# A planned attention and feed-forward kernel: urgencies corrected by two tables, two buffers laid out by block, and a plan that knows PSUM turns and the port

## The chip, the cores and the metric

The kernel runs on one core of one Trainium2 chip. The metric is device time in microseconds of that core; a run is one execution of the whole program. Engines are named as in the profile: PE (TensorE, the matrix engine), DVE (VectorE), ACT (ScalarE), POOL (GpSimd) and SP, whose queue issues every DMA of this kernel.

## What is computed

Chunked attention, whose output is the input of a gated feed-forward layer. Shapes: 8 batches, 8 heads, 576 positions, head size 64, so 4608 rows of 512; chunks of 64 positions; the feed-forward layer is 1024 wide.

```python
scores = q_chunk @ k_chunk.T / 8              # 64x64 for each chunk and head
attn = exp(scores - max) ; attn /= sum + 1e-9
x = attn @ v_chunk                            # heads side by side: rows of 512
h = maximum(x @ w_in, 0)                      # 512 -> 1024
conv[s] = cw[0]*h[s-1] + cw[1]*h[s] + cw[2]*h[s+1]   # zero beyond a batch
out = (h * sigmoid(conv)) @ w_out             # 1024 -> 512
```

The weights w_in, conv_w and w_out come as 64-bit floats; q, k and v as 32-bit floats.

## The kernel before

**Split products.** Each large product is made of three matrix products of shortened 32-bit numbers: high by high, high by low, low by high. So w_in, w_out, x and the gated g each exist as a pair of tiles in SBUF (`wi_h`/`wi_l`, `wo_h`/`wo_l`, `x_h`/`x_l`, `g_h`/`g_l`).

**Weights.** A 64-bit weight arrives as two 32-bit words in one of six raw slots (named `qk` in the profile, since rows of q and k use the same slots). The chain `split` turns one 512 KB piece into its high and low part: on DVE `w_mask` (L334), `w_rest` (L343), `w_low` (L347), `w_sign` (L352) or `w_one` (L358), and `w_pow` (L369); on ACT `w_bias` (L339), and `w_hi` (L362) where POOL doesn't make the high part with `w_hi_one` (L365); then mostly `w_lo_big` on POOL (L377) and `w_lo_copy` on ACT (L380). There are 8 pieces of w_in, 8 of w_out and a small one for conv_w. Before the change a piece of w_in is all 512 rows by 128 columns.

**Attention.** 36 tiles of 128 rows (two chunks). For each: rows of q and k are turned (`t_pe` on PE, L143, and `t_copy` on ACT, L147, for the first 9 tiles; `t_dve` on DVE, L152, for the others); `scores` on PE (L162); `s_max` (L172) and `s_sub` (L176) on DVE; `s_exp` on ACT (L181); `s_sum`, `s_eps`, `s_rec` on DVE (L185, L188, L191); `s_norm` on POOL (L194); `p_pe` (L201) and `p_copy` (L206); `attn_v` on PE (L214); then `x_hi` on ACT (L238) and `x_lo` on DVE (L242) write x. Scores and attention output share one PSUM tile, `sx_ps`, of two banks: scores lie in the first half of each bank, the output in the second half. The tile framework lets PE write a bank and DVE or ACT read it only one after the other.

**Feed-forward.** 16 units of 288 rows (half a batch). For each unit and each of 8 blocks of 128 columns: `mm1` on PE (L252, 12 matmuls over 290 columns; three PSUM buffers `h_ps`), then `h_relu`, `c_mid`, `c_sig` and `g_hi` on ACT (L258, L263, L278, L290), `c_left`, `c_right`, `c_mul` on DVE (L267, L273, L281) and `g_lo` on POOL (L294). x is a ring of three units. `mm2` on PE (L305) adds, for each of 36 output tiles, 8 steps of 3 matmuls; `o_copy` (L310) and `o_store` follow. Exp and sigmoid need different tables in ACT, so the profile shows table loads at L181 and L278.

**The order.** Nothing runs in the order in which it is written. Every piece of work is a `step` with an engine, an estimated cost, a key (its urgency), the steps it comes after, and the buffers that it takes and frees. A planner in the kernel's own Python (L567 to L650) plays the steps out engine by engine: among the ready steps of an engine, those that could start within 0.15 us of the earliest are candidates, and the lowest key wins. The steps are then issued in the planned order, and a dependency from each instruction to the one before it on its engine fixes that order. On the chip every engine works through its own list in that order and waits at each step for what the step needs.

The planner's DVE and POOL steps marked `port` share a port: when the other engine holds it, the planner before lengthens the step's cost, after the step is picked. It doesn't know that scores and attention output take turns in the two banks of `sx_ps`.

Of the kernel before, what the change touches and what calls it, by code (L numbers as in the profile page):

```python
# [30 lines left out]
def attn_ffn(ctx: ExitStack, tc: tile.TileContext, q, k, v, w_in, conv_w, w_out, out):  # L31
# [48 lines left out]
    wi_h = const.tile([P, KT, DF], F32R, name="wi_h")  # L80
    wi_l = const.tile([P, KT, DF], F32R, name="wi_l")
# [139 lines left out]
    def x_views(st, t, x):  # L221

        xv = sx[:, :, G * C:2 * G * C].rearrange("p s (g i) -> p g s i", i=C)
        parts = []
        for s in range(2):
            b, t0 = chunk(2 * t + s)
            for half, lo, hi in ((0, 0, HS + 2), (1, HS - 2, S)):
                i, j = max(lo, t0), min(hi, t0 + C)
                if i < j:
                    parts.append((s, i - t0, j - i, XU * ((2 * b + half) % NX) + i - lo))  # L230
        if [p[1:3] for p in parts] == [(0, C)] * 2 and parts[1][3] == parts[0][3] + C:
            o = parts[0][3]
# [12 lines left out]
    def mm1(st, u, f):  # L245

        o = XU * (u % NX)
        st["h"] = h_ps = ps_h.tile([P, 512], F32, name="h_ps")
        n = 0
        for wt, xt in ((wi_h, x_h), (wi_h, x_l), (wi_l, x_h)):  # L250
            for kt in range(KT):
                nc.tensor.matmul(  # L252
                    h_ps[:, 0:XU], lhsT=wt[:, kt, P * f:P * f + P], rhs=xt[:, kt, o:o + XU],
                    start=n == 0, stop=n == 3 * KT - 1)
                n += 1
# [180 lines left out]
    def att(t, key, load_key, exps, writes):  # L436
# [150 lines left out]
    while any(ready.values()):  # L587
        best = None
        for e, cand in ready.items():
            picks = []  # L590
# [94 lines left out]
```

## Time and profile before

| | us |
|---|---|
| median of 3 runs | 554.38 |
| lowest, highest | 553.79, 557.0 |
| the profiled execution, device time | 554.14 |
| its span, first to last instruction | 552.4 |

A profile shows one execution. The span is shorter than the device time by what lies around it, 1.74 us. "Busy" is the share of time in which an engine had an instruction of the kind; PE's weight loads are kept apart as PEld. A group row gives a line, engine, operation, output and inputs, the count, the total and mean time, and the idle time of the engine just before the group with what ended it. PE's matmuls overlap, so the time that one costs is the distance between two starts, not its own length: the length holds the way through the array too.

Three stages can be told apart. In the first there is no `mm1`; in the second the weights are still being split; from about 109 us on all weights are ready, and PE alternates between `mm1`, `mm2` and short excursions to the attention of later tiles.

### The profile page before, as it was taken

How to read it: one execution, taken by the hardware profiler on the slowest of the kernel's cores; microseconds unless marked ns; L12 is line 12 of the kernel's file. 1: busy time of each engine (PE TensorE's matmuls, PEld its weight loads, DVE VectorE, ACT ScalarE, POOL GpSimd, SP SyncE). 2: the span in 40 equal slices, each digit the busy share in tenths (PEclk: the TensorE clock that was granted, in tenths of full speed). 3: DMA queues.
4: the chain of work that ended last, by engine and by line, in shares of the span. 5: the costliest groups of instructions: out<-in, count | busy, mean ns of one | idle time of the engine just before them, and what ended most of it. 6: DMA issues, size and time to landing. Idle time of an engine off the chain costs nothing.

```text
span 552.4 us, 12919 instructions
## 1 busy us (share of the span) xinstructions
PE 507.9 (92%) x4921; PEld 435.8 (79%) x4921; DVE 373.8 (68%) x760; ACT 365.6 (66%) x819; POOL 183.2 (33%) x250
## 2 busy tenths in 40 slices
PE   3567678899999999999999999999999999999997
PEld 2456567788888878887888889797888888788985
DVE  4898979866868477475777656675877656655530
ACT  3558977767794667757594845767685845768641
POOL 0454644632341323322341421232342422232420
PEclk9979979999999999999999999999999999999999
DMA  8997650145324555423355551333352101000001
GB/s 191 243 222 208 165 118 1 40 96 93 64 48 106 90 121 107 99 58 72 82 95 103 106 106 50 58 80 70 81 104 68 39 20 40 1 20 21 21 38 58
DMA packets 185314, 47.03 MB, mean 85 GB/s; under 512 B 175500, under 2 KB 179620, under 8 KB 185252
## 3 DMA queue, kind: packets, MB, share of 16 engines
q1 hardware_dynamic: 185252, 46.20, 37.9%
q8 instruction: 39, 0.64, 0.5%
q14 instruction: 23, 0.19, 0.1%
HBM read 36.72 MB, written 9.44 MB: 84 GB/s over the span
## 4 chain that ended last, share of the span: by engine, by line
PE 74%; DVE 10%; ACT 8%; issue 2%; POOL 2%; DMA 2%; SPq 2%; POOLq 0%; ACTq 0%; DVEq 0%
PE o_ps L305 32%; PE h_ps L252 29%; PE sx_ps L214 4%; PE sx_ps L162 4%; PE pt_ps L201 3%; ACT L181 3%; POOL e L194 2%; DMA qk<-in_k 2%; DVE z L185 2%; ACT e L181 1%; PE h_ps L143 1%; DVE wv L347 1%; ACT c L263 1%; ACT h_ps L258 1%; ACT x_h L238 1%
## 5 line engine op out<-in xcount | busy, mean ns | idle before, releaser
L294 POOL TENSOR_TENSOR g_l<-c,g_h 128x288 fp32r<-128x288 f32 (+8 forms) x184 | 113.4, 630 | 245.4 <-ACT g_h L290 231.1
L305 PE MATMUL o_ps<-wo_h,g_h 128*128 128x512 f32 x288 | 120.4, 418 | 0.0
L305 PE MATMUL o_ps<-wo_l,g_h 128*128 128x512 f32 x288 | 113.6, 394 | 4.2 <-ACT wo_l L380 4.2
L267 DVE SCALAR_TENSOR_TENSOR c<-h_ps,cw,c 128x288 f32<-128x288 f32 (+1 forms) x128 | 65.1, 509 | 72.2 <-ACT c L263 72.2
L305 PE MATMUL o_ps<-wo_h,g_l 128*128 128x512 f32 x288 | 113.8, 395 | 0.0
L252 PE MATMUL h_ps<-x_h,wi_h 128*128 128x290 f32 x512 | 91.5, 301 | 5.3 <-DVE c L281 5.3
L252 PEld LDWEIGHTS h_ps<-x_h,wi_h 128*128 128x128 f32 x512 | 81.7, 191 | 16.5 <-DVE c L281 4.0
L278 ACT ACTIVATE c<-c 128x288 f32<-128x288 f32 x128 | 55.7, 444 | 57.4 <-DVE c L273 56.1
L252 PE MATMUL h_ps<-x_l,wi_h 128*128 128x290 f32 x512 | 91.1, 301 | 0.0
L252 PE MATMUL h_ps<-x_h,wi_l 128*128 128x290 f32 x512 | 90.1, 298 | 0.0
L281 DVE TENSOR_TENSOR c<-h_ps,c 128x288 f32<-128x288 f32 x128 | 56.9, 452 | 34.6 <-ACT c L278 34.0
L252 PEld LDWEIGHTS h_ps<-x_l,wi_h 128*128 128x128 f32 x512 | 76.7, 191 | 0.4 <-DVE x_l L242 0.3
L252 PEld LDWEIGHTS h_ps<-x_h,wi_l 128*128 128x128 f32 x512 | 76.5, 191 | 0.0
L290 ACT CAST g_h<-c 128x288 fp32r<-128x288 f32 (+8 forms) x184 | 59.4, 358 | 24.5 <-DVE c L281 23.0
L263 ACT ACTIVATE c<-h_ps,cw 128x288 f32<-128x288 f32 x128 | 64.0, 500 | 9.3 <-POOL g_l L294 0.4
L258 ACT ACTIVATE h_ps<-h_ps 128x290 f32<-128x290 f32 x128 | 50.8, 397 | 29.1 <-PE h_ps L252 27.9
L273 DVE SCALAR_TENSOR_TENSOR c<-h_ps,cw,c 128x287 f32<-128x287 f32 (+1 forms) x128 | 66.1, 517 | 4.2
L305 PEld LDWEIGHTS o_ps<-wo_h,g_l 128*128 128x128 f32 x288 | 54.3, 188 | 12.4
L305 PEld LDWEIGHTS o_ps<-wo_l,g_h 128*128 128x128 f32 x288 | 54.4, 189 | 10.4 <-ACT wo_l L380 5.2
L305 PEld LDWEIGHTS o_ps<-wo_h,g_h 128*128 128x128 f32 x288 | 54.4, 189 | 7.5
L194 POOL TENSOR_TENSOR e<-e,z 128x512 f32<-128x512 f32 x36 | 37.9, 1052 | 57.3 <-DVE z L191 42.1
L214 PEld LDWEIGHTS sx_ps<-pT,v 64*64 64x64 f32 x1152 | 21.8, 143 | 20.6 <-issue 8.0
(53 smaller groups left out, 549.5 us busy)
## 6 DMA issues: line engine op xcount, KB each, us to landing
v<-in_v SPq DMA_DIRECT2D x144, 64.0 KB, 2.7
out<-o_sb SPq DMA_DIRECT2D x36, 256.0 KB, 2.2
qk<-in_q SPq DMA_DIRECT2D x96, 48.0 KB, 2.3
qk<-in_k SPq DMA_DIRECT2D x96, 48.0 KB, 2.3
qk<-in_moe_w_in SPq DMA_DIRECT2D x8, 512.0 KB, 5.2
qk<-in_moe_w_out SPq DMA_DIRECT2D x8, 512.0 KB, 5.3
qk<-in_q SPq DMA_DIRECT2D x96, 24.0 KB, 1.9
qk<-in_k SPq DMA_DIRECT2D x96, 24.0 KB, 1.9
```

Source lines behind the costliest of these rows:

```text
L194: nc.gpsimd.tensor_tensor(out=st["e"], in0=st["e"], in1=st["z"].rearrange("p (h o) -> p h o", o=1).broadcast_to([P, H, C]), op=ALU.mult)
L214: nc.tensor.matmul(x_ps[D * hp:D * hp + D, s, C * g:C * g + C], lhsT=st["v"][j0:j0 + C, g, s, :], rhs=st["pT"][j0:j0 + C, g, C * s:C * s + C],
L252: nc.tensor.matmul(h_ps[:, 0:XU], lhsT=wt[:, kt, P * f:P * f + P], rhs=xt[:, kt, o:o + XU], start=n == 0, stop=n == 3 * KT - 1)
L258: nc.scalar.activation(out=st["h"][:, 0:XU], in_=st["h"][:, 0:XU], func=AF.Relu)
L263: nc.scalar.mul(out=st["c"], in_=st["h"][:, i0:i0 + HS], mul=cw[:, FT + f:FT + f + 1])
L267: nc.vector.scalar_tensor_tensor(out=c[:, a:HS], in0=st["h"][:, i0 + a - 1:i0 + HS - 1], scalar=cw[:, f:f + 1], in1=c[:, a:HS], op0=ALU.mu ...
L273: nc.vector.scalar_tensor_tensor(out=c[:, 0:b], in0=st["h"][:, i0 + 1:i0 + 1 + b], scalar=cw[:, 2 * FT + f:2 * FT + f + 1], in1=c[:, 0:b], ...
L278: nc.scalar.activation(out=st["c"], in_=st["c"], func=AF.Sigmoid)
L281: nc.vector.tensor_tensor(out=st["c"], in0=st["h"][:, st["i0"]:st["i0"] + HS], in1=st["c"], op=ALU.mult)
L290: nc.scalar.copy(out=g_h[:, f, gs], in_=st["c"][:, cs])
L294: nc.gpsimd.tensor_tensor(out=g_l[:, f, gs], in0=st["c"][:, cs], in1=g_h[:, f, gs].bitcast(F32), op=ALU.subtract)
L305: nc.tensor.matmul(st["o"], lhsT=gt[:, f, o:o + P], rhs=wt[:, f, :], start=f == 0 and n == 0, stop=f == FT - 1 and n == 2)
```

## The change

The added and removed code works at five places.

1. *Urgencies.* After all steps are made, two tables are added to the keys: `by_step` by the function's name, and `by_chain` by the chain of steps that share a state (one tile, one block, one weight piece). A search over plans made the numbers; a row of such a table says nothing by itself.
2. *The planner's rules.* A step on the shared port now starts only when the other engine has let go of the port (it waits in the plan, and another step may be picked). A step in the bank pair "sx" waits until the other engines' steps in that pair have ended. The window of candidates is 0.6 us instead of 0.15, and starting late costs 32 key points for each us. The first ACT step pays for a table load, and only ACT steps change the loaded table. Some costs of loads are raised.
3. *x by units.* `x_h` and `x_l` go from (4 row groups, 3 units x 290) to (3 units, 4 row groups, 290), so that what belongs to a unit lies together. Two chunks are written by one instruction only where both lie in one unit.
4. *w_in by blocks.* `wi_h` and `wi_l` go from (4, 1024) to (4 block pairs, 4, 256). A piece of w_in is now half of the rows by 256 columns, so two pieces are needed before the two blocks of a pair can start.
5. Loads, results and arithmetic are otherwise the same.

The core of the diff:

```diff
-    x_h = const.tile([P, KT, NX * XU], F32R, name="x_h")
+    x_h = const.tile([P, NX, KT, XU], F32R, name="x_h")
-    wi_h = const.tile([P, KT, DF], F32R, name="wi_h")
+    wi_h = const.tile([P, FT // 2, KT, 2 * P], F32R, name="wi_h")
...
-    src_i = [w_in.rearrange("(k p) f -> p k f", p=P)[:, :, 2 * P * f:2 * P * f + 2 * P] for f in range(FT)]
+    src_i = [w_in.rearrange("(k p) f -> p k f", p=P)[:, 2 * (n % 2):2 * (n % 2) + 2, 4 * P * (n // 2):4 * P * (n // 2) + 4 * P] for n in range(FT)]
...
+        for f in (n - n % 2, n - n % 2 + 1):
+            wi_done[f] = wi_done.get(f, []) + list(ends)
...
+    by_step = {
+        "w_bias": 3, "w_rest": 1.5, "w_sign": 1, "w_pow": -1.5, "w_hi": 5, "w_lo": 2.5, "w_one": 0.5, "w_hi_one": 1,
...
+    by_chain = [
+        -27, -43, -2, -2, -3, 12, 14, 1, -9, -107, 2, 2, 7, 5, 1, 0, 1, 11, -3, -1, -1, -7, -4, 11, -10, -9, 3, 1, 4,
...
+        s["key"] += by_step.get(name, 0.0) + by_chain[chains.setdefault(a, len(chains))] / 2
...
+                    if s["port"]:
+                        t = max(t, port[other[e]] - share[e])
+                    for o, until_ in bank.get(s["bank"], {}).items():
+                        if o != e:
+                            t = max(t, until_ + late[e])
...
-                t, _, i = min((p for p in picks if p[0] <= t + 0.15), key=lambda p: p[1])
+                t, _, i = min((p for p in picks if p[0] <= t + 0.6), key=lambda p: p[1] + 32 * (p[0] - t))
...
-            cost += max(0.0, port[other] - t - (0.2 if e == "DVE" else 0.137))
```

How this moves instructions shows at three places. The rows are in the order of one engine's list. Line numbers between 76 and 242 of the kernel before are one higher after the change.

The first is PE's list after the fourth unit, around the attention of tiles 12 to 14: L201 is `p_pe`, L214 `attn_v`, L162 `scores`, L305 a third of an `mm2` step, L252 a third of an `mm1`. Before, from `p_pe` of tile 12 on:

```order
L201 MATMUL pt_ps<-ident,e 128x128 x4
L305 MATMUL o_ps<-wo_h,g_h 128x512
L305 MATMUL o_ps<-wo_l,g_h 128x512
L305 MATMUL o_ps<-wo_h,g_l 128x512
L214 MATMUL sx_ps<-pT,v 64x64 x16
L201 MATMUL pt_ps<-ident,e 128x128 x4
L162 MATMUL sx_ps<-kT,qT 64x64 x16
L305 MATMUL o_ps<-wo_h,g_h 128x512
L305 MATMUL o_ps<-wo_l,g_h 128x512
L305 MATMUL o_ps<-wo_h,g_l 128x512
L214 MATMUL sx_ps<-pT,v 64x64 x16
```

After, from `attn_v` of tile 12 on (`scores` of tile 14 and `p_pe` of tile 12 stand three `mm2` steps earlier):

```order
L215 MATMUL sx_ps<-pT,v 64x64 x16
L202 MATMUL pt_ps<-ident,e 128x128 x4
L252 MATMUL h_ps<-x_h,wi_h 128x290 x4
L252 MATMUL h_ps<-x_l,wi_h 128x290 x4
L252 MATMUL h_ps<-x_h,wi_l 128x290 x4
L163 MATMUL sx_ps<-kT,qT 64x64 x16
L215 MATMUL sx_ps<-pT,v 64x64 x16
L252 MATMUL h_ps<-x_h,wi_h 128x290 x4
L252 MATMUL h_ps<-x_l,wi_h 128x290 x4
L252 MATMUL h_ps<-x_h,wi_l 128x290 x4
```

Between `attn_v` of one tile and `scores` of another there was only a `p_pe`, and between those `scores` and the next `attn_v` one `mm2` step; now a whole `mm1` lies between the first two, and `scores` and `attn_v` stand back to back.

The second is DVE's list at the first `mm1` blocks, while weights are split: L334, L343, L347, L358 and L369 are the weight chain; L172 is `s_max`, L176 `s_sub`, L185 `s_sum`, L267 and L273 `c_left` and `c_right`. Before:

```order
L172 TENSOR_REDUCE m<-sx_ps 128x8
L176 TENSOR_TENSOR e<-sx_ps,m 128x2x4x64
L369 TENSOR_SCALAR we<-wi_h 128x512
L334 TENSOR_SCALAR o_sb<-qk 128x512
L343 TENSOR_SCALAR wv<-qk 128x512
L267 SCALAR_TENSOR_TENSOR c<-h_ps,cw,c 128x287
L273 SCALAR_TENSOR_TENSOR c<-h_ps,cw,c 128x288
```

And the same stretch after:

```order
L173 TENSOR_REDUCE m<-sx_ps 128x8
L334 TENSOR_SCALAR o_sb<-qk 128x512
L358 TENSOR_SCALAR ws<-qk 128x512
L369 TENSOR_SCALAR we<-wi_h 128x512
L177 TENSOR_TENSOR e<-sx_ps,m 128x2x4x64
L267 SCALAR_TENSOR_TENSOR c<-h_ps,cw,c 128x287
L273 SCALAR_TENSOR_TENSOR c<-h_ps,cw,c 128x288
L186 TENSOR_REDUCE z<-e 128x8
L343 TENSOR_SCALAR wv<-qk 128x512
L369 TENSOR_SCALAR we<-wi_h 128x512
```

`w_rest` (L343) stood right behind `w_mask` (L334) and `w_pow`; now `s_sub`, `c_left`, `c_right` and `s_sum`, none of them marked for the port, stand ahead of it.

The third is the head of SP's list, the first loads. Before:

```order
L322 DMA qk<-in_moe_w_in 128x4x256
L103 DMA qk<-in_q 128x8x64
L103 DMA qk<-in_k 128x8x64
L135 DMA v<-in_v 64x4x64 x4
L322 DMA qk<-in_moe_w_in 128x4x256
L103 DMA qk<-in_q 128x8x64
```

After:

```order
L322 DMA qk<-in_moe_w_in 128x2x512 x2
L322 DMA qk<-in_moe_conv_w 24x256
L104 DMA qk<-in_q 128x8x64
L104 DMA qk<-in_k 128x8x64
L136 DMA v<-in_v 64x4x64 x4
L104 DMA qk<-in_q 128x8x64
```

Two pieces of w_in and conv_w now go ahead of the first rows of q, where one piece of w_in went before.

More of the change, by code (lines that the diff above doesn't have):

```diff
@@ L64, in attn_ffn, with step @@
     steps = []
-    def step(eng, cost, key, fn, args=(), after=(), take=(), free=(), lag=0.0, table=None, port=False):
+    def step(eng, cost, key, fn, args=(), after=(), take=(), free=(), lag=0.0, table=None, port=False, bank=None):
         s = dict(eng=eng, cost=cost, key=key, fn=fn, args=args, after=[a for a in after if a], take=take, free=free,
-                 lag=lag, table=table, port=port)
+                 lag=lag, table=table, port=port, bank=bank)
         steps.append(s)
@@ L454, in att @@
         tt[0]["after"] += [before["T"]] if t else []
-        s = step("PE", 0.47, key, scores, (st,), tt + [before.get("s")], take=["s"], free=["qT", "kT"])
+        s = step("PE", 0.47, key, scores, (st,), tt + [before.get("s")], take=["s"], free=["qT", "kT"], bank="sx")
         before.update(v=ldv, T=tt[1], s=s)
-        s = step("DVE", 0.69, key, s_max, (st,), [s], take=["m"])
-        s = step("DVE", 0.68, key, s_sub, (st,), [s], take=["e"], free=["m", "s"])
+        s = step("DVE", 0.69, key, s_max, (st,), [s], take=["m"], bank="sx")
+        s = step("DVE", 0.68, key, s_sub, (st,), [s], take=["e"], free=["m", "s"], bank="sx")
         exps.append(s)
@@ L467, in att @@
         s = step("ACT", 0.59, key + 12, p_copy, (st,), [s], take=["pT"], free=["pt"])
-        s = step("PE", 0.47, key + 14, attn_v, (st,), [s, ldv], take=["x"], free=["pT", "v"])
+        s = step("PE", 0.47, key + 14, attn_v, (st,), [s, ldv], take=["x"], free=["pT", "v"], bank="sx")
         n = len(x_views(st, t, x_h)) - 1
-        s = step("ACT", 0.58 + 0.15 * n, key + 14, x_hi, (st, t), [s] + writes)
-        return step("DVE", 0.69 + 0.1 * n, key + 14, x_lo, (st, t), [s], free=["x"])
+        s = step("ACT", 0.58 + 0.15 * n, key + 14, x_hi, (st, t), [s] + writes, bank="sx")
+        return step("DVE", 0.69 + 0.1 * n, key + 14, x_lo, (st, t), [s], free=["x"], bank="sx")
     group_loads, before = {}, {}
@@ L560, in attn_ffn @@
             step("SP", 0.5, key + 2, o_store, (st, t), [s], free=["o_sb"], lag=0.8)
+    by_step = {
+        "w_bias": 3, "w_rest": 1.5, "w_sign": 1, "w_pow": -1.5, "w_hi": 5, "w_lo": 2.5, "w_one": 0.5, "w_hi_one": 1,
+        "w_lo_copy": -1, "c_sum": 11, "c_pe": -1, "c_copy": 8.5, "load_rows": -0.5, "t_pe": 3, "t_copy": -3, "scores":
+        -2.5, "s_sub": 5, "s_exp": 1, "s_sum": 1, "s_eps": -0.5, "s_rec": -1, "s_norm": 4.5, "p_pe": 2.5, "p_copy": 7.5,
+        "attn_v": 2.5, "x_lo": 4.5, "h_relu": 3.5, "c_left": 1.5, "c_right": 0.5, "c_sig": 0.5, "c_mul": 1.5, "g_hi":
+        4.5, "g_lo": 9, "o_copy": -6, "o_store": 4, "load_group": -2, "load_part": 5, "t_dve": 8
+    }
+    by_chain = [
[9 rows of a table added]
+    ]
+    chains = {}
+    for s in steps:
+        a, name = s["args"][0] if s["args"] else None, s["fn"].__name__
+        a = id(a) if isinstance(a, dict) else ("load" if name.startswith("load") else name, a)
+        s["key"] += by_step.get(name, 0.0) + by_chain[chains.setdefault(a, len(chains))] / 2
     early = {"DVE": 0.083, "ACT": 0.092, "PE": 0.0, "POOL": -0.075, "SP": -0.05}
@@ L577, in attn_ffn @@
     free_at["SP"] = 0.7
-    port = {"DVE": 0.0, "POOL": 0.0}
-    dma_free, table, pe_f32 = 0.0, "exp", False
+    port, other, share = {"DVE": 0.0, "POOL": 0.0}, {"DVE": "POOL", "POOL": "DVE"}, {"DVE": 0.2, "POOL": 0.137}
+    dma_free, table, pe_f32, bank = 0.0, None, False, {}
     left = [len(a) for a in befores]
@@ L617, in attn_ffn @@
         s, cost = steps[i], steps[i]["cost"]
-        table = s["table"] or table
+        if e == "ACT":
+            table = s["table"] or table or "exp"
         if e == "PE":
```

36 lines of the change are left out of this document (18 added, 18 removed), and 8 rows, old and new, of the table by_chain.

## The prediction

> **What bounds the kernel now.** I read the page's first part and then the busy time by stage. The stages end at the first `mm1` (39.4 us), at the last weight operation of DVE (108.8) and at the last `mm1` (529.5). The columns are the stretch, its length, and busy time with instruction count of PE, PEld, DVE, ACT and POOL, then granted clock, DMA share and GB/s.
>
> ```profile
> PE 507.9 (92%) x4921; PEld 435.8 (79%) x4921; DVE 373.8 (68%) x760; ACT 365.6 (66%) x819; POOL 183.2 (33%) x250
> ...
> 0.00:39.40 39.40, 20.52 (x277) 15.59 (x278) 29.07 (x60) 19.56 (x35) 13.30 (x17) 0.95 0.91 218
> 39.40:108.80 69.40, 54.56 (x542) 47.34 (x541) 61.93 (x119) 54.83 (x111) 38.52 (x34) 0.93 0.46 113
> 108.80:529.50 420.70, 413.54 (x4023) 357.36 (x4022) 280.81 (x579) 286.24 (x661) 129.22 (x196) 1.00 0.34 70
> ```
>
> In the second stage DVE is busy for 61.93 of 69.40 us while PE idles for 14.8: DVE's weight chains set the pace there. In the third PE is busy for 413.54 of 420.70 and bounds the time. So the change is worth something in two ways: less DVE time lost before 108.8, and less PE time lost after it. How much PE loses in the third stage the busy share hides, since pipelined matmuls overlap. I take the counts there, and the distance between starts.
>
> ```profile
> L305 PE MATMUL o_ps<-wo_h,g_h 128*128 128x512 f32 x247 | 103.6, 419 | 0.0
> ...
> L252 PE MATMUL h_ps<-x_l,wi_h 128*128 128x290 f32 x444 | 78.1, 298 | 0.0
> ...
> L214 PE MATMUL sx_ps<-pT,v 64*64 64x64 f32 x928 | 20.2, 224 | 3.8 <-issue 3.1 <-ACT pT L206 0.7
> L162 PE MATMUL sx_ps<-kT,qT 64*64 64x64 f32 x896 | 19.4, 224 | 0.6
> L201 PE MATMUL pt_ps<-ident,e 128*128 128x128 f32 x116 | 18.8, 285 | 0.9
> ```
>
> The chain that ended last gives one `mm2` step (3 matmuls) as 19.25/28 = 0.69 us and one `mm1` (12) as 3.23/2 = 1.61.
>
> ```profile
> 509.81 3.23 PE h_ps L252 x24
> ...
> 529.56 19.25 PE o_ps L305 x84
> ```
>
> PE's timeline around a lone `scores` shows what an excursion from the wide matmuls to attention costs.
>
> ```profile
> 210.05 0.40 PE L305 MATMUL o_ps<-wo_l,g_h 128*128 128x512 f32 x1
> 210.29 0.40 PE L305 MATMUL o_ps<-wo_h,g_l 128*128 128x512 f32 x1
> 210.62 0.69 PE L162 MATMUL sx_ps<-kT,qT 64*64 64x64 f32 x32
> 211.24 0.51 PE L305 MATMUL o_ps<-wo_h,g_h 128*128 128x512 f32 x1
> 211.58 0.40 PE L305 MATMUL o_ps<-wo_l,g_h 128*128 128x512 f32 x1
> ```
>
> One mm2 matmul takes 0.69/3 = 0.23, so `scores` starts 0.10 late (0.33 after the start before it); it takes 0.62, and the matmul behind it 0.34 instead of 0.23. An excursion costs 0.21 beyond its own work.
>
> The third stage then holds 444/12 = 37 times three kinds, that is 111 `mm1`, 247 `mm2` steps, 29 `attn_v` (928/32), 28 `scores` and 29 `p_pe`: 179 + 170 + 18 + 17 + 10 (a `p_pe` at 0.35, the distance of two starts below), and about 1 for one last transpose, makes 395. Of 420.7 us, about 25 are lost. PE's list has 66 excursions from the 17th `mm1` on: 66 x 0.21 = 13.9. The other 11 or so are stalls, and this timeline of all engines shows the commonest, a turn in the PSUM banks of `sx_ps`:
>
> ```profile
> 199.48 0.69 PE L214 MATMUL sx_ps<-pT,v 64*64 64x64 f32 x32
> 200.11 0.66 PE L201 MATMUL pt_ps<-ident,e 128*128 128x128 f32 x4
> 200.25 0.59 ACT L238 CAST x_h<-sx_ps 128x512 fp32r<-128x512 f32 x1 [0.41 <-PE sx_ps L214]
> 200.89 0.69 PE L162 MATMUL sx_ps<-kT,qT 64*64 64x64 f32 x32
> ...
> 202.09 0.39 PE L305 MATMUL o_ps<-wo_h,g_l 128*128 128x512 f32 x1
> 202.33 0.68 DVE L172 TENSOR_REDUCE m<-sx_ps 128x8 f32<-128x512 f32 x1
> ...
> 203.11 0.69 PE L214 MATMUL sx_ps<-pT,v 64*64 64x64 f32 x32 [0.63 <-issue]
> ```
>
> `scores` could have started at 200.11 + 0.35 + 0.10 = 200.56; it starts at 200.89, when `x_hi` has left the bank (200.84). The next `attn_v` could have started at 202.32; it starts at 203.11, behind `s_max` (203.01). One such knot costs 0.33 + 0.79 = 1.12 us.
>
> **The change part by part.** The sum is made against the profiled execution, 554.14 us; the median of the runs is 554.38, 0.24 more.
>
> *Bank turns known to the plan.* The list before has five knots of this kind (tiles 12, 16, 23, 25 and 32); the list after has one `attn_v` as close behind `scores` (one 0.69 step), worth 0.8 as above, and two at 1.39 us of work, just short of what `s_max` and its like take twice (0.68 each, and the starts between), worth 0.1 each. Gain 5 x 1.12 - 1.0 = 4.6. Now `scores` often stands right behind `attn_v`: `x_hi` waits 0.62 longer, queued behind it on ACT are `p_copy` and conv work, and the next unit's first `mm1` waits for x. That `mm1` now mostly stands 2.9 us of PE work behind the unit's last `attn_v`, against 2.1 before, so the longer wait is covered.
>
> *Fewer excursions.* 66 become 48: 18 x 0.21 = 3.8.
>
> *`attn_v` close behind its `p_pe`.* With one `mm2` step between, it came 0.13 late (199.48, where the last matmul at 199.12 allowed 199.35).
>
> ```profile
> 198.21 0.60 PE L201 MATMUL pt_ps<-ident,e 128*128 128x128 f32 x4
> 198.56 0.48 PE L305 MATMUL o_ps<-wo_h,g_h 128*128 128x512 f32 x1
> ...
> 199.12 0.40 PE L305 MATMUL o_ps<-wo_h,g_l 128*128 128x512 f32 x1
> ```
>
> 7 such places become 3: 0.5.
>
> *x by units.* Before, an access to one unit spanned its neighbours' columns, and the built program has waits across units. One shows: `x_hi` waits for an `mm1` of another unit, `p_copy` queues behind it on ACT, and `attn_v` behind that.
>
> ```profile
> 224.79 0.70 PE L252 MATMUL h_ps<-x_h,wi_l 128*128 128x290 f32 x4
> ...
> 225.39 0.59 ACT L238 CAST x_h<-sx_ps 128x512 fp32r<-128x512 f32 x1 [1.11 <-PE h_ps L252]
> ...
> 226.85 0.70 PE L214 MATMUL sx_ps<-pT,v 64*64 64x64 f32 x32 [0.65 <-ACT pT L206]
> ```
>
> That is 0.65; six `mm1` with such a wait elsewhere show some 0.05 each. Gain 1.0. Three more tiles are written in two pieces on ACT and DVE, each piece shorter: under 1 us in all, on engines with 134 us of slack in the third stage. Nothing.
>
> *New stalls.* A new order can have stalls that the old one hadn't. I bound this by nothing and by one knot for each of the five removed (5.6), and take 1.0, nearer the lower end since the new list has one short turn.
>
> Third stage: 4.6 + 3.8 + 0.5 + 1.0 - 1.0 = 8.9 gained.
>
> *The port, in the first two stages.* DVE's groups up to 108.8 us (mean ns of one behind the total):
>
> ```profile
> L347 DVE SCALAR_TENSOR_TENSOR wv<-qk,wv 128x512 f32<-128x512 uint32 x16 | 11.7, 733 | 0.2
> L343 DVE TENSOR_SCALAR wv<-qk 128x512 uint32<-128x512 uint32 x16 | 11.4, 715 | 0.0
> L334 DVE TENSOR_SCALAR o_sb<-qk 128x512 uint32<-128x512 uint32 x16 | 10.4, 648 | 4.4 <-DMA qk<-in_moe_w_in 4.4
> ...
> L188 DVE TENSOR_SCALAR z<-z 128x8 f32<-128x8 f32 x7 | 3.7, 531 | 0.2
> ...
> L358 DVE TENSOR_SCALAR ws<-qk 128x512 uint32<-128x512 uint32 x8 | 3.3, 415 | 0.0
> ```
>
> And three rows of the timeline:
>
> ```profile
> 40.30 1.39 POOL L377 TENSOR_TENSOR wv<-wv,we 128x512 f32<-128x512 f32 x1 [0.80 <-DVE we L369]
> ...
> 40.48 1.50 DVE L343 TENSOR_SCALAR wv<-qk 128x512 uint32<-128x512 uint32 x1
> ...
> 219.52 0.17 DVE L188 TENSOR_SCALAR z<-z 128x8 f32<-128x8 f32 x1
> ```
>
> L358 is the same form as L343 and L334 and never waits: 415 ns. The excess is 16 x 0.300 + 16 x 0.233 = 8.5 us, and L188, which takes 0.17 when alone (219.52), adds 7 x 0.36 = 2.5: 11.0 us. The cause is POOL: L343 at 40.48 ends 0.29 after POOL's instruction, having taken 1.50 for its 0.42.
>
> The Trainium skill ("SBUF — State Buffer", section "🔬 SBUF: two separate sides") says that DVE and GpSimd share a port pair as an exclusive lock, held for the whole instruction, and that the loser blocks. The trace agrees, with the 1.50 us above. The rule speaks against this gain: a lock is waited for wherever the instruction stands, unless other work fills the wait. By it alone the sum would be that of the third stage, 545.2, and it stands among the rivals.
>
> Bounds from the rows: all 11.0 gained, or nothing gained and 3.6 lost, since DVE now has 39.5 us of uncontended work listed ahead of the first `c_mul`, against 35.9 (each kind counted with its time where it did not wait). ACT's table loads give a middle: two fewer by the last weight piece.
>
> ```profile
> L278 ACT ACT_TABLE_LOAD x3 | 3.8, 1283 | 0.1
> ```
>
> Two loads are 2.6 us of ACT; with a tenth of the port's 11.0 I take 3.7, the low half, since weight work ahead of the 17th `w_pow` is unchanged (87.5 us of uncontended DVE work before, 89.8 after, with one block more done).
>
> *w_in by blocks* costs nothing in bytes; the first q rows come one 512 KB piece later, while DVE has a second weight chain to do. *The tail* keeps PE's last `mm2` run (32 steps now, not 28, the same total).
>
> Sum: 554.14 - 8.9 - 3.7 = 541.5 us, 2.3% under the median.
>
> **The rivals.**
>
> *The port's waits stay.* DVE asks for the port as often as before, and POOL holds it as long: each L343 put later meets another POOL instruction, and the first two stages gain nothing: 554.14 - 8.9 = 545.2. This is the lock of the page named above. For it: POOL is busy for 38.52 of 69.40 us in the second stage.
>
> *The waits are filled.* DVE has other work for them (`s_sub`, `c_left` now stand there). Then all 11.0 go: 554.14 - 8.9 - 11.0 = 534.2. Against it: the same 38.52 us, and DVE's list keeps many port instructions in a row.
>
> *Stalls move.* Bank waits return elsewhere (`x_hi` behind `scores`, DVE and ACT in strict order), and only the excursions are gained: 554.14 - 3.8 = 550.3. For it: PE's list depends on estimated costs; against it: the knots were seen one by one and are gone from the list.
>
> *The change doesn't do what it says*: costs of the plan differ from those of the chip, so removed and new waits balance: 554.
>
> *Slower: paired blocks.* Both blocks of a pair need two weight chains, so at each of the four pairs PE could wait for one chain more: three DVE instructions like L358 and two like L347 (2.7), one on POOL like that at 40.30 (1.39), and one on ACT:
>
> ```profile
> L380 ACT ACTIVATE wi_l<-wv 128x512 fp32r<-128x512 f32 x7 | 4.4, 630 | 3.0 <-POOL wv L377 2.9
> ```
>
> That is 4.7 us. Four times: 18.8, so 554.14 - 8.9 + 18.8 = 564.0. It decides once the four add more than 12.6 together, against the 8.9 + 3.7 gained. Against it: the first `mm1` waits for x of tile 2 anyway; by then both lists hold 7 begun chains.
>
> **How the numbers follow.** Forecast 541.5 (536 to 548) 0.38; port stays 0.14; port filled 0.15; moved stalls 0.18; no effect 0.08; paired blocks 0.07. A measurement of this kernel can tell about 1% from no change. Under 548.8 lie the first three and part of the third (0.07), so faster 0.74; slower, over 559.9, is the last, 0.07; the rest 0.19 is the same. The range 531 to 553 reaches below the filled port by some 3 us, for new stalls that don't come (1.0) and table loads (2.6), and above the moved stalls, and leaves out the paired blocks and most of no effect.
>
> **What would show it.** Right: the third stage has `attn_v` rows with less idle time than 3.8 on PE, and no `scores` that starts right after an `x_hi`; L343 and L334 nearer 415 ns; weights done before 105 us. Wrong: the last weight operation after 112, PE idling at the first `mm1` blocks, or new waits of the first `mm1` of a unit for `x_lo`.

## The result, and the profile after

| | before | after |
|---|---|---|
| median, us | 555.67 (4 runs, 553.79 to 557.0) | 533.81 (4 runs, 533.46 to 534.47) |
| profiled execution, us | 554.14 | 533.55 |
| its span, us | 552.4 | 531.8 |

The ratio is 0.961, with a 95% interval from 0.9573 to 0.9648: 3.9% faster. The prediction said 541.5 us within 531 to 553, so side and range held. The narrower band that it gave to its own sum, 536 to 548, did not hold: the gain was 20.6 us of span where 12.6 were forecast, and the time lies where its rival "the waits are filled" (534.2) was.

The stages of the kernel after, cut as in the prediction (first `mm1`, last weight operation of DVE, end of the last `mm1`), in the same columns, with the page's first part above them:

```profile
PE 500.3 (94%) x4921; PEld 437.6 (82%) x4921; DVE 364.6 (69%) x763; ACT 359.4 (68%) x818; POOL 184.9 (35%) x250
...
0.00:37.70 37.70, 19.95 (x309) 15.60 (x309) 28.81 (x62) 20.73 (x37) 13.59 (x17) 0.99 0.89 226
37.70:99.50 61.80, 54.18 (x520) 47.50 (x518) 56.55 (x120) 51.56 (x112) 40.41 (x34) 0.92 0.57 133
99.50:505.70 406.20, 403.71 (x4002) 356.95 (x4001) 276.85 (x576) 282.09 (x659) 128.36 (x195) 1.00 0.34 71
505.70:531.80 26.10, 22.42 (x96) 17.56 (x95) 2.40 (x5) 5.07 (x12) 2.57 (x6) 1.00 0.13 49
```

The first two stages fell from 108.8 to 99.5 us, the third from 420.7 to 406.2, and the rest grew from 22.9 to 26.1, because PE's last run has 96/3 = 32 `mm2` steps instead of 28 (2.8 of the 3.2 us). So 9.3 us came in the first two stages, and some 14.5 - 2.8 = 11.7 us for the same work in the third. TensorE's mean granted clock is 0.988 before and 0.990 after, so it is not what makes the difference. PE's groups of the third stage:

```profile
L305 PE MATMUL o_ps<-wo_h,g_h 128*128 128x512 f32 x244 | 99.1, 406 | 0.0
...
L252 PE MATMUL h_ps<-x_l,wi_h 128*128 128x290 f32 x444 | 78.1, 298 | 0.0
...
L215 PE MATMUL sx_ps<-pT,v 64*64 64x64 f32 x928 | 20.0, 224 | 0.0
L163 PE MATMUL sx_ps<-kT,qT 64*64 64x64 f32 x896 | 18.9, 222 | 1.9 <-DVE kT L153 1.9
L202 PE MATMUL pt_ps<-ident,e 128*128 128x128 f32 x116 | 18.4, 281 | 0.1
```

`attn_v` (L215, L214 before) lost its 3.8 us of idle time. One new stall is in sight, 1.9 us at a `scores`. DVE's groups of the first two stages, up to 99.5 us:

```profile
L347 DVE SCALAR_TENSOR_TENSOR wv<-qk,wv 128x512 f32<-128x512 uint32 x16 | 12.6, 789 | 0.2
L343 DVE TENSOR_SCALAR wv<-qk 128x512 uint32<-128x512 uint32 x16 | 7.2, 448 | 0.0
L334 DVE TENSOR_SCALAR o_sb<-qk 128x512 uint32<-128x512 uint32 x16 | 7.1, 442 | 7.1 <-DMA qk<-in_moe_w_in 5.7 <-DMA v<-in_v 1.4
...
L358 DVE TENSOR_SCALAR ws<-qk 128x512 uint32<-128x512 uint32 x8 | 3.7, 460 | 0.0
...
L189 DVE TENSOR_SCALAR z<-z 128x8 f32<-128x8 f32 x7 | 1.9, 276 | 0.0
...
L374 DVE SCALAR_TENSOR_TENSOR wi_l<-wv,we 128x512 fp32r<-128x512 f32 x1 | 1.6, 1642 | 0.0
...
L374 DVE SCALAR_TENSOR_TENSOR we<-wv,we 24x128 f32<-24x128 f32 x1 | 1.4, 1384 | 0.0
```

Of the excess of 11.0 us at the port, 16 x 0.033 + 16 x 0.027 + 7 x 0.106 = 1.7 us is left in the three groups L343, L334 and L189 (L188 before). Other DVE steps of the weight chain got longer, though: L347 takes 789 ns where it took 733, L358 460 where it took 415, and the two of L374 took 692 and 279 ns in the same view of the kernel before. So the 9.3 us that these three groups lost are not all saved; what DVE saves in total is read below, beside e1.

### The profile page after: what moved, and what is told of

Same layout as the page of the kernel before. It is cut to its first block, busy times and chain, and to the rows that moved or that the text cites. A ratio compares the mean times of both kernels' runs of the same rounds, so it can differ in the third digit from the quotient of the medians.

```text
span 531.8 us, 12836 instructions
## 1 busy us (share of the span) xinstructions
PE 500.3 (94%) x4921; PEld 437.6 (82%) x4921; DVE 364.6 (69%) x763; ACT 359.4 (68%) x818; POOL 184.9 (35%) x250
## 4 chain that ended last, share of the span: by engine, by line
PE 78%; SPq 7%; DVE 6%; ACT 5%; DMA 3%; issue 1%; POOL 0%; ACTq 0%; DVEq 0%; POOLq 0%
PE o_ps L305 34%; PE h_ps L252 34%; SPq L124 4%; PE sx_ps L215 3%; PE sx_ps L163 3%; PE pt_ps L202 3%; PE h_ps L144 1%; SPq L136 1%; DMA qk<-in_moe_w_in 1%; DMA v<-in_v 1%; ACT c L263 1%; DVE c L267 1%; ACT L278 1%; DVE c L281 1%; DVE c L273 1%
## 5 line engine op out<-in xcount | busy, mean ns | idle before, releaser
L305 PE MATMUL o_ps<-wo_h,g_h 128*128 128x512 f32 x288 | 116.9, 406 | 0.6 <-ACT wo_h L362 0.6
L305 PE MATMUL o_ps<-wo_l,g_h 128*128 128x512 f32 x288 | 113.9, 395 | 2.3 <-ACT wo_l L380 2.2
L305 PE MATMUL o_ps<-wo_h,g_l 128*128 128x512 f32 x288 | 113.9, 395 | 0.0
L267 DVE SCALAR_TENSOR_TENSOR c<-h_ps,cw,c 128x288 f32<-128x288 f32 (+1 forms) x128 | 65.6, 513 | 62.3 <-ACT c L263 61.4
L252 PE MATMUL h_ps<-x_h,wi_h 128*128 128x290 f32 x512 | 94.1, 307 | 4.5 <-DVE c L281 4.2
L252 PE MATMUL h_ps<-x_l,wi_h 128*128 128x290 f32 x512 | 91.3, 301 | 0.0
L252 PEld LDWEIGHTS h_ps<-x_h,wi_h 128*128 128x128 f32 x512 | 79.8, 192 | 13.8 <-DVE c L281 6.9
L252 PE MATMUL h_ps<-x_h,wi_l 128*128 128x290 f32 x512 | 90.5, 299 | 0.0
L252 PEld LDWEIGHTS h_ps<-x_l,wi_h 128*128 128x128 f32 x512 | 77.5, 193 | 0.0
L252 PEld LDWEIGHTS h_ps<-x_h,wi_l 128*128 128x128 f32 x512 | 77.2, 192 | 0.0
L273 DVE SCALAR_TENSOR_TENSOR c<-h_ps,cw,c 128x288 f32<-128x288 f32 (+1 forms) x128 | 65.7, 515 | 3.5
L305 PEld LDWEIGHTS o_ps<-wo_h,g_l 128*128 128x128 f32 x288 | 54.2, 188 | 12.4 <-POOL g_l L294 0.2
L305 PEld LDWEIGHTS o_ps<-wo_l,g_h 128*128 128x128 f32 x288 | 54.3, 188 | 11.0 <-ACT wo_l L380 3.2
L305 PEld LDWEIGHTS o_ps<-wo_h,g_h 128*128 128x128 f32 x288 | 54.3, 189 | 10.4 <-ACT wo_h L362 0.8
L195 POOL TENSOR_TENSOR e<-e,z 128x512 f32<-128x512 f32 x36 | 39.3, 1092 | 64.5 <-DVE z L192 56.4
L310 ACT COPY o_sb<-o_ps 128x512 f32<-128x512 f32 x36 | 21.0, 584 | 33.0 <-PE o_ps L305 32.4
```

What stands on the lines that cost most here:

```text
L195: nc.gpsimd.tensor_tensor(out=st["e"], in0=st["e"], in1=st["z"].rearrange("p (h o) -> p h o", o=1).broadcast_to([P, H, C]), op=ALU.mult)
L252: nc.tensor.matmul(h_ps[:, 0:XU], lhsT=wt[:, f // 2, kt, P * (f % 2):P * (f % 2) + P], rhs=xt[:, u % NX, kt, :], start=n == 0, stop=n == 3 ...
L267: nc.vector.scalar_tensor_tensor(out=c[:, a:HS], in0=st["h"][:, i0 + a - 1:i0 + HS - 1], scalar=cw[:, f:f + 1], in1=c[:, a:HS], op0=ALU.mu ...
L273: nc.vector.scalar_tensor_tensor(out=c[:, 0:b], in0=st["h"][:, i0 + 1:i0 + 1 + b], scalar=cw[:, 2 * FT + f:2 * FT + f + 1], in1=c[:, 0:b], ...
L305: nc.tensor.matmul(st["o"], lhsT=gt[:, f, o:o + P], rhs=wt[:, f, :], start=f == 0 and n == 0, stop=f == FT - 1 and n == 2)
```

## The experiments

Theory 1: the tables carry most of the gain, through the order of work. Theory 2: the planner's rules for port and banks carry it. All kernels in one table; "17th" is the start of the 17th `mm1`, after which TensorE bounds the time, and "rest" goes from there to the end. In before's order 274 `mm2` steps are left at that point, in after's (also e3, e4, e7, e11) 276, which is 1.4 us more work. The ratio is to the kernel before on the same chip (553.6 to 554.7 us beside the experiments); microseconds of different rows can come from different chips.

| kernel | median us | ratio (95% interval) | first mm1 | 17th | rest |
|---|---|---|---|---|---|
| before | 555.67 | | 39.4 | 107.5 | 444.9 |
| after | 533.81 | 0.961 (0.9573 to 0.9648) | 37.7 | 96.9 | 434.9 |
| e1_no_tables | 550.77 | 0.9934 (0.9907 to 0.9961) | 45.8 | 109.6 | 439.8 |
| e2_layouts_only | 556.68 | 1.0046 (1.001 to 1.0082) | 40.6 | 107.4 | 446.5 |
| e3_x_ring | 537.79 | 0.9706 (0.968 to 0.9732) | 36.5 | 95.8 | 438.4 |
| e4_wi_rows | 532.96 | 0.9634 (0.9601 to 0.9667) | 37.7 | 96.2 | 434.2 |
| e5_port_only | 549.91 | 0.9904 (0.9874 to 0.9935) | 39.0 | 104.4 | 443.7 |
| e6_bank_only | 549.70 | 0.9893 (0.9862 to 0.9924) | 40.4 | 110.5 | 437.8 |
| e7_tables_early | 536.89 | 0.9659 (0.9632 to 0.9685) | 37.9 | 96.4 | 439.1 |
| e8_tables_late | 550.67 | 0.9926 (0.9901 to 0.9952) | 43.0 | 107.8 | 437.7 |
| e9_port_and_bank | 546.82 | 0.9863 (0.9832 to 0.9893) | 39.6 | 104.7 | 439.3 |
| e10_old_dma_costs | 545.84 | 0.9851 (0.982 to 0.9882) | 39.6 | 106.5 | 439.8 |
| e11_group_earlier | 534.63 | 0.964 (0.9613 to 0.9667) | 37.5 | 95.9 | 436.2 |
| e12_rest_twice | 559.07 | 1.0072 (1.0042 to 1.0102) | 41.1 | 112.5 | 447.0 |

### The tables: e1, e7, e8

e1, from the kernel after:

```diff
-        s["key"] += by_step.get(name, 0.0) + by_chain[chains.setdefault(a, len(chains))] / 2
+        s["key"] += 0.0
```

> The changed kernel with both tables of key corrections left out: the new layouts and all of the planner's new rules and costs stay, each step keeps its plain urgency. Theory 1 (the tables carry the gain: they close up the float32 excursions of TensorE, 66 to 48 after the 17th mm1, and order VectorE's weight work): most of the 21.9 us comes back, 547 to 557 us; the weights are ready near 108 us again, and TensorE idles some 7 us in the third stage. Theory 2 (the planner's rules for the port and the banks carry it): the time stays at 531 to 540 us, the weights ready before 102 us. In this kernel 59 excursions are left after the 17th mm1, so by the excursions alone it would lose 11 x 0.21 = 2.3 us to the changed kernel.

The kernel is 17.0 us slower than the one after, and of the 3.9% gained 0.7% is left: theory 1. The way is not the expected one: 12.7 us come back ahead of the 17th `mm1` and 4.9 behind it. Stretches up to the 17th `mm1` of e1, then the second one of after and of before:

```profile
0.00:45.80 45.80, 23.31 (x309) 17.02 (x309) 29.30 (x63) 21.46 (x38) 15.99 (x18) 1.00 0.84 202
45.80:109.60 63.80, 52.66 (x471) 46.20 (x467) 55.53 (x114) 49.98 (x108) 35.64 (x32) 0.89 0.45 112
```

```profile
37.70:96.90 59.20, 51.58 (x504) 45.07 (x502) 54.14 (x116) 49.64 (x107) 38.75 (x33) 0.92 0.56 134
```

```profile
39.40:107.50 68.10, 53.26 (x533) 46.04 (x532) 60.63 (x117) 54.51 (x111) 37.52 (x34) 0.93 0.47 114
```

DVE is busy for 29.07 + 60.63 = 89.7 us before, for 29.30 + 55.53 = 84.8 in e1 and for 28.81 + 54.14 = 83.0 in after. So without the tables 4.9 us of DVE's work are saved already, and the 17th `mm1` is later all the same, since DVE idles for 109.6 - 84.8 = 24.8 us instead of 107.5 - 89.7 = 17.8. With the tables it idles for 96.9 - 83.0 = 13.9 us: they take 10.9 us of idle time, and 1.8 of work. The waits of DVE in the first two stages (total, times, longest), e1 and then after, show where:

```profile
DVE m L173 <- PE sx_ps L163: 8.4, 5, 2.6
DVE o_sb L334 <- DMA qk<-in_moe_w_in: 5.6, 2, 5.4
```

```profile
DVE o_sb L334 <- DMA qk<-in_moe_w_in: 5.7, 2, 4.7
DVE m L173 <- PE sx_ps L163: 1.8, 2, 1.3
```

`s_max` waits for `scores`, and TensorE for rows. In e1's timeline the transposes of tile 4 stand ahead of the first `mm1` on PE and wait for its rows; those are issued on SP at 33.40, behind the four loads of v of tiles 0 to 3:

```profile
40.72 1.09 PE L144 MATMUL h_ps<-ident,qk 128*128 128x128 f32 x4 [2.17 <-DMA qk<-in_q]
42.99 1.09 PE L144 MATMUL h_ps<-ident,qk 128*128 128x128 f32 x4 [1.19 <-DMA qk<-in_k]
44.76 1.13 PE L163 MATMUL sx_ps<-kT,qT 64*64 64x64 f32 x32 [0.67 <-ACT kT L148]
45.81 0.61 PE L252 MATMUL h_ps<-x_h,wi_h 128*128 128x290 f32 x1
```

SP's timeline of the kernel after has the same rows at 22.70, behind two loads of v (about 5 us each):

```profile
3.31 4.91 SPq L136 DMA_DIRECT2D v<-in_v  x4
8.26 0.60 SPq L104 DMA_DIRECT2D qk<-in_q  x1
...
15.25 4.99 SPq L136 DMA_DIRECT2D v<-in_v  x4
...
22.70 1.28 SPq L104 DMA_DIRECT2D qk<-in_q  x2
```

e7 and e8 apply the tables to one part of the steps each (e8 with `>= 120`):

```diff
-        s["key"] += by_step.get(...) + by_chain[...] / 2
+        add = by_step.get(...) + by_chain[...] / 2
+        s["key"] += add if s["key"] < 120 else 0.0
```

> The changed kernel with its corrections applied only to steps whose plain key is under 120; the steps due later keep their plain keys. TensorE's order is the changed kernel's up to the 26th mm1; behind it 55 excursions instead of 48 are left after the 17th mm1. Theory 1 (the gains of the two parts stand apart, the tables carry both): the 17th mm1 starts near 97 us as in the changed kernel, and the third stage takes what the kernel without tables took, some 4 to 6 us more than the changed kernel's: 537 to 542 us. Rival (the early gain is given back later, since the late keys wait for other work anyway): 545 us or more.

> The changed kernel with its corrections applied only to steps whose plain key is 120 or more; the first two stages keep plain keys. Theory 1 (the gains of the two parts stand apart): the 17th mm1 starts near 108 to 110 us as in the kernel without tables (109.6 us), the third stage takes some 4 us less than that kernel's: 545 to 549 us. Rival (the first stages are carried by the rules and not by the tables, so they keep their gain): under 541 us. 53 excursions are left after the 17th mm1.

e7 is 13.9 us under e1 and keeps the 17th `mm1` at 96.4; after is another 3.1 under e7, in the rest (439.1 to 434.9; the intervals of the two ratios just overlap). e8 missed the 545 to 549 us of its theory: it is no better than e1 in the median (the intervals overlap). Its profile, of the shortest of its runs, has 107.8 and 437.7. Early and late corrections act at different places, as theory 1 has it, and the early ones are worth several times the late ones (13.9 against 3.1 us in the medians, 13.2 against 4.2 by stage); whether the late ones keep their 3 us without the early, e8 leaves open.

### The costs of loads: e10

e1 with the planner's former costs of loads:

```diff
-            ld = step("SP", 1.9, load_key, load_rows, ...
+            ld = step("SP", 1.25, load_key, load_rows, ...
-            end[i] = max(dma_free + 1.0, t + cost + 2.0)
+            end[i] = max(dma_free + 0.4, t + cost + 1.9)
```

and the lag of 1.65 for all weights.

> The changed kernel without its tables, and with the planner's former costs of loads (1.25 us instead of 1.9 for a tile's rows, the weights' lag of 1.65, and a landing 0.6 us earlier). Without tables the first mm1 began at 45.8 us, 6.4 us later than before, with 12.3 us of TensorE's idle time put down to loads of q. Theory (the new costs of loads alone push the rows of the first tiles behind weights, and the tables repair it): the first mm1 at 39 to 41 us, the time 543 to 547 us. Rival (the new choice among ready steps or the layouts do it): the first mm1 stays after 44 us and the time within 2 us of 550.8.

The first `mm1` is back at 39.6 and the time at 545.84: the theory. Without tables the raised costs of loads lose 4.9 us. So the new rules, window and layouts together are worth about 9 us on plain keys, the costs take 5 back, and the tables, on top of these costs, give 17. The tables with the former costs, or on the planner before, were not tried.

### The rules: e5, e6, e9

To the kernel before, e5 adds the first piece to the planner, e6 the second (with the `bank="sx"` marks and the line that records an end), e9 both:

```diff
+                    if s["port"]:
+                        t = max(t, port["POOL" if e == "DVE" else "DVE"] - (0.2 if e == "DVE" else 0.137))
...
+                    for o, until_ in bank.get(s["bank"], {}).items():
+                        if o != e:
+                            t = max(t, until_ + late[e])
```

> The kernel before with the planner's port rule alone: a step that takes the port isn't started before the other engine's step gives it free, so the planner puts other work there. Theory of the prediction (L343, L334 and L188 wait less, and a tenth of the 11.0 us of port excess comes off the path): 551 to 554 us, the mean of L343 well under 683 ns. Rival A (the waits at the port are on the path, the whole excess comes back): 543 to 548 us. Rival B (the waits only move: the planner knows them, but VectorE has nothing else that is due): the means stay within 10% and so does the time, 553 to 556 us. The order of TensorE hardly differs (65 excursions after the 17th mm1 instead of 66).

DVE's groups of e5, to the end of its weight work:

```profile
L343 DVE TENSOR_SCALAR wv<-qk 128x512 uint32<-128x512 uint32 x16 | 9.6, 602 | 0.0
L334 DVE TENSOR_SCALAR o_sb<-qk 128x512 uint32<-128x512 uint32 x16 | 9.0, 560 | 4.5 <-DMA qk<-in_moe_w_in 4.5
...
L188 DVE TENSOR_SCALAR z<-z 128x8 f32<-128x8 f32 x7 | 2.6, 367 | 0.1
```

Of the excess, 1.8 + 1.4 + 1.1 = 4.3 us are gone (from 715, 648 and 531 ns), and the 17th `mm1` is 3.1 us earlier: roughly 0.7 for each, not the prediction's tenth, and the time lies between its theory and rival A.

> The kernel before with the planner's bank rule alone: work on the bank of scores and attn_v isn't planned while another engine works on it. In the order of TensorE, 6 places are left at which scores and attn_v follow each other within 1.1 us of other work, instead of 11, and 65 excursions instead of 66. Theory (five knots at 1.1 us each are taken out by this rule, nothing else): 547 to 551 us, and the waits of 0.91 us in front of attn_v in the third stage gone. Rival (the knots go but their time comes back in other waits, since the keys were tuned without the rule): 553 to 557 us.

PE's groups of e6 in the third stage: the idle time of `attn_v` is 0.2 instead of 3.8.

```profile
L214 PE MATMUL sx_ps<-pT,v 64*64 64x64 f32 x928 | 20.1, 224 | 0.2 <-DVE x_l L242 0.2
```

The rest fell by 7.1 us, and 3.0 were lost ahead of the 17th `mm1`. The theory's time holds for the median (5.0 us less), and the removed turns are at least as large as priced; that the rule does nothing else does not hold, and why the first stages lost 3.0 us stays open.

> The kernel before with both planner rules, port and bank, and nothing else. The port rule alone was worth 4.7 us (first two stages 3.1), the bank rule alone 5.0 us (all in the third stage). Theory (the two work at different places and add): 544 to 546 us. Rival (the plan reacts to both at once and gives one of them back): 548 to 552 us. Left to the tables and the rest of the change would then be some 11 us.

Each stage has about what the rule at work in it gave alone: 104.7 us up to the 17th `mm1` (e5 104.4), and 439.3 for the rest (e6 437.8). In the medians 7.9 of 9.7 us came, between the two theories. e10, which beside both rules has the layouts, the wider window and the price of late starts, is at 545.84 against 546.82, within the intervals: on plain keys nothing beyond the two rules can be measured. The window was not tried alone.

### The price of VectorE time: e12

To the kernel before, in `w_rest`:

```diff
         nc.vector.tensor_scalar(
             out=st["V"].bitcast(U32), in0=st["H"], scalar1=0x1FF, scalar2=None, op0=ALU.bitwise_and)
+        nc.vector.tensor_scalar(
+            out=st["V"].bitcast(U32), in0=st["H"], scalar1=0x1FF, scalar2=None, op0=ALU.bitwise_and)
```

> The kernel before with VectorE's w_rest issued twice in a row, with the same inputs and the same output: 16 more instructions of 128x512, all in the first two stages, some 0.42 us each without a wait at the port, so 6.6 us more of VectorE there; the plan and all orders are as before. It prices a microsecond of VectorE in these stages. The prediction's choice (a tenth reaches the end): 0.7 us slower, 555 to 556 us. Rival (VectorE is the bound there, two thirds or more reach the end, as the port rule alone suggests: 4.4 us off the three waiting groups and 3.1 us off the stages): 4.4 to 7 us slower, 559 to 562 us.

DVE's groups (L345 is the added one) and the stretch between the first and the 17th `mm1`:

```profile
L343 DVE TENSOR_SCALAR wv<-qk 128x512 uint32<-128x512 uint32 x16 | 11.9, 744 | 0.0
...
L345 DVE TENSOR_SCALAR wv<-qk 128x512 uint32<-128x512 uint32 x16 | 9.0, 564 | 0.5
```

```profile
41.10:112.50 71.40, 56.58 (x532) 48.99 (x530) 66.51 (x127) 54.28 (x109) 36.74 (x32) 0.90 0.42 106
```

DVE is busy for 32.32 + 66.51 = 98.8 us up to the 17th `mm1`, 9.1 more than before, and that `mm1` is 5.0 us later: 0.55 us for each. This profile is of the longest run; the median is 4.4 us up (ratio 1.0042 to 1.0102, so 2.3 to 5.7 us), or 0.25 to 0.63 us for each of the 9.1. The tenth is out; the rival's two thirds are a little high.

### The layouts: e2, e3, e4

e2 puts both layouts, and nothing else, into the kernel before; e3 and e4 put the former layout of x, or of w_in, back into the kernel after, whose order they keep:

```diff
-    x_h = const.tile([P, NX, KT, XU], F32R, name="x_h")
+    x_h = const.tile([P, KT, NX * XU], F32R, name="x_h")
```

```diff
-    wi_h = const.tile([P, FT // 2, KT, 2 * P], F32R, name="wi_h")
+    wi_h = const.tile([P, KT, DF], F32R, name="wi_h")
```

(`x_l` and `wi_l` and the accesses alike.)

> The kernel before with only the two layouts: x by units, w_in by blocks with each of its loads a half of the rows over twice the columns; planner, costs and keys as before. Theory of the prediction (waits on foreign units go, 1.0 us; a 2 KB packet of w_in costs nothing or helps a little): 552 to 555 us, 1 us or so under the kernel before. Rival (layouts carry a good part, through fewer packets or writes without waits): under 548 us. Rival (a mm1 now waits for the second of two loads, both needed by its block, and the plan that was made for single columns runs late): 556 to 562 us, with TensorE idle before the first mm1 units.

> The changed kernel's order with x_h and x_l laid out as before, one ring of columns for all units beside each other. Theory of the prediction (false waits between units cost about 1.0 us where the order was made without them): 534 to 536 us. Rival (the tight order of the changed kernel leans on the layout: x_hi and x_lo wait for mm1 of another unit, and attn_v behind them): 538 us or more, with x's writes idle before PE in the table of groups. Rival (no effect): 533.5 to 534.2 us.

> The changed kernel's order with wi_h and wi_l laid out by rows as before; the loads themselves stay as changed (half the rows, twice the columns). The split's writes are then 256 columns out of 1024, two rows of them, instead of one run of 512. Theory (the layout only spares false waits and does nothing for the speed of one write): 533.5 to 534.5 us, L343, L334 at the same mean of 442 to 448 ns. Rival (the layout makes the writes shorter or spares waits of mm1 on other blocks): 536 us or more, with the means of the split up by 5% or idle PE in front of L252 in the first units.

The layout of w_in does nothing that can be measured (532.96 against 533.81 us, the intervals overlap; L343 and L334 take 448 and 442 ns in both kernels). That of x is worth 4.0 us in the new order (the rest, 434.9 to 438.4): e3's 537.79 us lies above the theory's 534 to 536 and just under the rival's 538, and comes by the rival's way. Waits of e3 in its third stage:

```profile
DVE x_l L243 <- PE h_ps L252: 9.1, 6, 2.6
...
ACT x_h L239 <- PE h_ps L252: 5.8, 4, 1.9
...
PE h_ps L252 <- ACT x_h L239: 1.2, 2, 0.7
...
PE sx_ps L215 <- DVE x_l L243: 0.7, 1, 0.7
```

None of these four is in the same view of the kernel after: x waits there for no `mm1`. In the old order (e2) the two layouts gained nothing: 0.1 to 0.8% slower, with the 17th `mm1` where it was (107.4) and the rest 1.6 us longer. The wait that the prediction showed is gone there all the same: `attn_v` has 3.2 us of idle time in e2's third stage, and the 0.7 behind `p_copy` is not among them. Which of the two layouts costs the 1.6 was not parted.

### The stall that is left: e11

```diff
     group_key = {j: key_of[TG * j] - 30 for j in range(NAT // TG, NT // TG)}
+    group_key[21 // TG] -= 8
```

> The changed kernel with the loads of one group of three tiles (tiles 21 to 23) due 8 us earlier. In the changed kernel SyncE issues loads without a pause from 217 to 273 us, and scores of tile 21 wait 1.87 us for DVE's transposes of k, which wait for the last load of that group, the only wait over half a us left in the third stage. Its issue moves ahead of a load of v and of a store, some 3 us earlier. Theory (the wait is a late issue and nothing else): 1.5 to 2.2 us faster than the changed kernel, 531.5 to 532.5 us. Rival (the load of v that is passed, or the next group, is then late): 533.5 to 535 us with a new wait of TensorE at attn_v or scores behind 260 us.

No measurable difference from after (the intervals overlap), and the wait grew, at the same `scores`; PE's timeline of e11:

```profile
272.52 0.69 PE L163 MATMUL sx_ps<-kT,qT 64*64 64x64 f32 x32 [2.86 <-DVE kT L153]
```

The edit moved the whole group a little and not the loads that are late. In SP's timeline of the kernel after, the last two parts of this group (x8 each) stand behind all eight parts of the next one (x4 each):

```profile
241.99 3.83 SPq L124 DMA_DIRECT2D qk<-in_k  x8
245.91 3.13 SPq L124 DMA_DIRECT2D qk<-in_q  x4
...
261.38 2.00 SPq L124 DMA_DIRECT2D qk<-in_k  x4
263.48 0.41 SPq L313 DMA_DIRECT2D out<-o_sb  x1
263.94 5.14 SPq L124 DMA_DIRECT2D qk<-in_q  x8
269.13 3.83 SPq L124 DMA_DIRECT2D qk<-in_k  x8
```

In e11 the two parts still stand behind the next group: its timeline has that last issue at 267.94, only 1.2 us earlier, and TensorE arrives 1.6 us earlier. To put the two parts ahead of the next group wasn't tried. None of the experiments beats the kernel after by more than the intervals (e4, the nearest, overlaps with it).

## Why the prediction was right, and where its sizes were wrong

*What bounds each stage.* Right. TensorE bounds the third stage (403.71 busy of 406.20 after), and VectorE's work weighs on the first two (e12). The signs that the prediction named came too: the weights are done at 99.5 us, L343 and L334 are near 415 ns, `attn_v` has no idle time, and PE waits at no `scores` for `x_hi` and at no `mm1` for x in the third stage.

*The turns in the banks (4.6).* Right, and rather small: `attn_v` lost its idle time, and with this rule alone the rest fell by 7.1 us (e6), which holds the five knots (5.6), the one wait of 0.65 that was put down to x, and about 1 us that is not assigned.

*Fewer excursions (3.8), `attn_v` close behind `p_pe` (0.5).* Consistent, not shown alone. From e6 to after the rest fell by 437.8 - 434.9 = 2.9 us with 1.4 us more work, and the order has 17 excursions fewer: 4.3 us against 17 x 0.21 = 3.6. Other waits changed too. The 0.5 counts something twice: of the 0.13 at which `attn_v` came late, 0.10 is the late start that is already in the 0.21 of an excursion, so by the prediction's own rows 4 x 0.03 = 0.1 is left.

*x by units (1.0).* The mechanism was right, the size was not: 3.5 to 4.0 us in the new order (e3). The term was read from the waits of the old order, which had been made around the false ones; there the layouts gained nothing (e2).

*New stalls (1.0 lost).* One came, 1.9 us. Idle time of PE in the third stage fell from 7.2 to 2.5 us all the same.

*The port, in the first two stages (3.7).* This is the step that failed: "with a tenth of the port's 11.0 I take 3.7, the low half". 9.3 us came, and the 17th `mm1` is 10.6 earlier. First, a microsecond of VectorE there is worth about half a microsecond (0.55 in e12, roughly 0.7 in e5) and not a tenth. Second, the three groups lost 9.3 of their 11.0 us of waits; since other steps take longer, DVE's busy time up to the 17th `mm1` fell by 6.7 us (89.7 to 83.0). At e12's price that is an estimated 3.7 us, where the tenth was 1.1. Third, the step had no term for idle time, and by this estimate the other 6.9 us are there: in e12 DVE's idle time fell by 4.1 us as its work grew by 9.1, so with less work it should have grown, and it fell from 17.8 to 13.9. What e1 and e10 show is that the order of loads on SP and of the first tiles moves it: without the tables it is 24.8 us (e1), and 18.3 with the former costs of loads (e10). The 2.6 us of the middle are not shown: ACT does load two tables fewer by the last weight operation (4 instead of 6), but e5 has only 4 as well, and what they are worth was never measured alone.

The rival "the waits are filled" came out at 534.2 us. Its sum is right only by chance: it gave all 11.0 us of the three groups back in full, where DVE saved 6.7 at about half price, it had no idle time, and it had too little in the third stage (8.9 against 11.7 for the same work). e1 shows that fewer waits alone gain nothing in the first stages when the loads come late: its three groups have 573, 573 and 311 ns, and its 17th `mm1` is 2.1 us later than before. (In the sum of the chances, "part of the third" means the moved stalls, the fourth of the list.)

The Trainium skill ("SBUF — State Buffer", section "🔬 SBUF: two separate sides") has the loser at the shared port blocked for the whole instruction. The traces agree that the wait is there: before, L343 takes 715 ns where L358 takes 415. By that rule alone, with nothing in the waits' place, the time would have been 545.2; a plan that knows the lock took 4.3 of the 11.0 us away (e5), and the kernel after 9.3 in the three groups. So how much is waited depends on where the instructions stand.

*The paired blocks* (564.0) did not come. In the page's table of groups of the kernel after, the idle time ahead of `mm1` is put down to `c_mul`, which frees its bank, and not to a weight:

```profile
L252 PE MATMUL h_ps<-x_h,wi_h 128*128 128x290 f32 x512 | 94.1, 307 | 4.5 <-DVE c L281 4.2
```

*The tail* is as forecast, 32 steps.

## What to carry to other kernels

Price a microsecond of a busy engine by doubling one of its instructions before a gain on it is written off or counted in full: here it was about half, not a tenth, and read what the whole engine saves, not only the groups that were priced. Where only an order changes, read the order of the DMA queue at the start as closely as that of the engines: here, on plain keys, the planner's costs of loads alone moved the first wide matmul by 6.2 us (e10, e1). And a dependency that is wider than the data cost nothing measurable in the order that was made around it and 4.0 us in the tight one, so test a layout with the order that it is meant for.

## What the runs showed of the hardware that was not expected

The same four DMA issues of a tile's v hold SP's queue for 4.91 us at 3.31 us (above) and for 2.57 at 45.83, as the timeline of the kernel after shows:

```profile
45.83 2.57 SPq L136 DMA_DIRECT2D v<-in_v  x4
```

The planner has one cost for both. And of two equal DVE instructions in a row (e12) the first took 744 ns in the mean and the second 564, still 149 over the 415 of one that never waits: being behind another DVE instruction does not always spare the port's wait. Three of the sixteen second ones took long (0.91, 1.39 and 1.15 us), each beside an instruction of POOL.
